# One pair's transposes on TensorE, and five weight pieces by casting DMAs, in a thresholded attention with a tanh-shrink MLP

## The chip, the cores and the metric

The kernel runs on one core of a Trainium2 chip. A core has five engines with queues of their own: TensorE (PE, with its weight loads PEld), VectorE (DVE), ScalarE (ACT), GpSimd (POOL) and SyncE (SP), which only issues DMAs here. Each engine takes its instructions in order; semaphores order the engines among each other. Sixteen DMA engines move data for all queues. The metric is the time of one execution on the device in microseconds, as a median of several runs.

## The reference, cut to what matters

```python
# q, k, v: (8, 8, 576, 64) float32; tau = 0.02
scores = (q @ k^T) / 8
thresh = max(scores, axis=-1) - tau
attn   = softmax(where(scores >= thresh, scores, -1e9))
x      = (attn @ v), heads side by side        # (4608, 512)
h      = x @ w_in                              # w_in (512, 2048)
out    = (h - tanh(h)) @ w_out                 # w_out (2048, 512)
```

## The kernel before, in words

**Attention.** The 64 (batch, head) couples are taken as 32 pairs of heads, counted from 0 in the code: the "eighth pair" is p = 7, the ninth p = 8. A pair has 2 x 576 query rows, nine tiles of 128 rows (`TPP = 9`), one of which, the shared one, holds the last 64 rows of both heads. Tiles are numbered through, i = 0 to 287; an even tile and the odd one after it make a duo. For a tile the kernel

1. computes the scores on TensorE, in PSUM (`scores`, L401 and L410). q and k are split into two float16 halves, kT holds a pair's transposed k and kS the same with the halves swapped, so that two rounds of matmuls give the float32-like product;
2. copies them to SBUF on VectorE, with the row maximum (L420), and derives the shift of a duo (`shift`, L432);
3. masks on ScalarE with a steep Prelu into z, bfloat16, the duo's two tiles side by side (`kink`, L447);
4. turns z so that keys lie on partitions. `on_pe(i)` decides: on TensorE by 128x128 transposes into PSUM (L466), four for the first tile of a duo and five for the second, each followed by an exp from PSUM (L475); or for the whole duo by one DMA transpose on SP's queue (zT, L454), followed by one exp (L483). PSUM tile psZ is double for the first four pairs and from then on shares the one buffer of psY;
5. multiplies by v on TensorE (`attend`, L506 to L524) and normalises on VectorE (`norm`). `emit_x` turns a pair's result on TensorE into xT.

**Preparation of a pair.** `load`/`load_part` bring q, k and v (up to the eighth pair on SP's queue, later on ScalarE's). `split` makes the float16 halves on GpSimd (three instructions, L228 to L232). `turn` transposes: on TensorE with a copy out of PSUM by VectorE (L284, L327), or by a DMA transpose on SP's queue (L315). `q_by_dma(p)` and `k_by_dma(p)` decide. `swap` makes kS from kT on GpSimd (two copies, L337), `split_v` casts v (L261 to L266).

**The MLP.** Per batch the hidden layer runs on TensorE in 16 steps (`hidden`, L579, psH), tanh on ScalarE (L592), the difference on VectorE (L598), and the second matrix in quarters (`project`, L605, psY). The first batch's hidden steps are mixed with the attention from step 40 on, by a written pattern.

**Weights.** w_in and w_out are loaded in eight pieces each (`w_load`): 512 KB of float32 into one of four buffers wt on SP's queue, and later a cast to bfloat16 on GpSimd (`w_cast`, L731).

**Order.** It is written out by hand: a loop over steps s = -8, -7, ... (L852) emits for each step its scores (tile s + 8), masks, turns and exps, MLP steps, attends, and then what `plan` lists for that step (loads, splits, turns, by leads before the pair's first tile: `LEADS`, `LATER`, `FIRST_LATER`), casts and weight loads. The lists `load_when` and `cast_when` hold steps counted from -8:

```python
    load_when = [3, 8, 13, 18, 21, 25, 29, 34, 38, 42, 46, 49, 52, 55, 58, 61]
    cast_when = [11, 19, 27, 32, 36, 40, 44, 47, 50, 53, 56, 59, 62, 65, 68, 71]
```

For the ninth pair `FIRST_LATER[8]` sets q's split ten, q's turn five, k's split eight and k's turn seven steps ahead.

Of the kernel before, what the change touches and what calls it, by code (L numbers as in the profile page):

```python
# [18 lines left out]
def kernel(  # L19
# [11 lines left out]
    nc = tc.nc  # L31
# [20 lines left out]
    TPP = 9  # L52
# [2 lines left out]


    def on_pe(i):
        p, j = divmod(i, TPP)
        return p < 6

    W = 2 * S

# [72 lines left out]
    DUAL = 8  # L135
# [167 lines left out]

    def q_by_dma(p):

        return p >= DUAL

    def k_by_dma(p):
        return p > DUAL
# [77 lines left out]
    def scores(i):  # L387
# [6 lines left out]
        if hh is None:  # L394
            qrem = REM
            if q_by_dma(p):
                qrem = (slice(512, 640, 2), slice(513, 640, 2))
            for n, kk in enumerate((kT, kS)):
                for dst, cols in ((main, main_keys), (rem, rem_keys)):
                    for hh in range(2):  # L400
                        nc.tensor.matmul(  # L401
                            out=ps[64 * hh : 64 * hh + 64, dst],
                            lhsT=qT[:, qrem[hh]], rhs=cols(p, kk, hh),
                            start=(n == 0), stop=(n == 1),
                        )
        else:
            lhs = qT[:, (5 * hh + t) * P : (5 * hh + t + 1) * P]
            for n, kk in enumerate((kT, kS)):
                for dst, cols in ((main, main_keys), (rem, rem_keys)):
                    nc.tensor.matmul(  # L410
                        out=ps[:, dst], lhsT=lhs, rhs=cols(p, kk, hh),
                        start=(n == 0), stop=(n == 1),
                    )
# [25 lines left out]
    def kink(i):  # L439
        sc, nb = scs.pop(i), nbs.pop(i)  # L440
        if kind(i) == "B":
            zt = zs.pop(i - 1)
            z = zt[:, S:W]
        else:
            zt = zs[i] = z_pool.tile([P, W], BF16, name="z")
            z = zt[:, 0:S]
        nc.scalar.activation(  # L447
            out=z, in_=sc, func=ACT.Prelu, bias=nb, scale=1.0, alpha=STEEP
        )
        if on_pe(i):  # L450
            zts[i] = zt
        elif kind(i) == "B":
            zts[i] = zt_pool.tile([P, TPP, P], BF16, name="zT")
            nc.sync.dma_start_transpose(out=zts[i], in_=zt)  # L454

    def weights(i):
# [4 lines left out]
        if on_pe(i):  # L461
            z = zts.pop(i)
            pl, tag = (ps_h, "h") if i % 2 and i < HPAIR * TPP else (ps_y, "y")
            ps = pl.tile([P, 5 * P], BF16, name="psZ", tag=tag)
            for c in range(n):
                nc.tensor.matmul(  # L466
                    out=ps[:, c * P : (c + 1) * P],
                    lhsT=z[:, (off + c) * P : (off + c + 1) * P],
                    rhs=ident_bf, is_transpose=True, start=True, stop=True,
                )  # L470
            if kd == "B":
                pt = pts.pop(i - 1)
            else:
                pt = p_pool.tile([P, TPP * P], FP16, name="pT")
            nc.scalar.activation(  # L475
                out=pt[:, off * P : (off + n) * P], in_=ps[:, 0 : n * P], func=ACT.Exp
            )
        elif kd == "A":
            return
        else:  # L480
            n += off
            pt = p_pool.tile([P, TPP * P], FP16, name="pT")
            nc.scalar.activation(  # L483
                out=pt[:, 0 : n * P], in_=zts.pop(i)[:, 0:n, :], func=ACT.Exp
            )
# [232 lines left out]
    def w_pieces():  # L718
        for w, sb, n in ((moe_w_in, w_in_sb, DM_C), (moe_w_out, w_out_sb, DF_C)):
            flat = sb.rearrange("p c n -> p (c n)")  # L720
            cols = n * w.shape[1] // 8
            src = w.rearrange("(c p) n -> p c n", p=P)

            for i in (0, 2, 4, 6, 1, 3, 5, 7) if w is moe_w_in else range(8):
                yield flat, src, i, cols, w.shape[1]
# [3 lines left out]
    def w_cast():  # L729
        flat, wt, i, cols = loaded.pop(0)  # L730
        nc.gpsimd.tensor_copy(out=flat[:, i * cols : (i + 1) * cols], in_=wt)  # L731

    def w_load(piece):
        flat, src, i, cols, width = piece
        wt = wt_pool.tile([P, cols], F32, name="wt", tag="wt")
        if cols >= width:
            r = cols // width
            s = src[:, i * r : (i + 1) * r, :]
            nc.sync.dma_start(out=wt.rearrange("p (c n) -> p c n", n=width), in_=s)
        else:  # L740
            r = width // cols
            s = src[:, i // r, (i % r) * cols : (i % r + 1) * cols]
            nc.sync.dma_start(out=wt, in_=s)
        loaded.append((flat, wt, i, cols))
# [53 lines left out]
    for p in range(1, DUAL):  # L798
        first = TPP * p - AHEAD
        for d, f in PREP[3 if p == 1 else 0 :]:  # L800
            d -= p == 1 and d == 3
            if p > HPAIR and d >= LDK - 2:
                d = ((16, 14, 12), (17, 15, 13))[1 - p % 2][LDK - d]
            elif d in (7, 8) and q_by_dma(p):
                d = ((9, 9) if d == 7 else (10, 10))[1 - p % 2]
            elif p in LEADS and d in (8, 7, 5, 4):
                d = LEADS[p][(8, 7, 5, 4).index(d)]
            elif d == 4:
                d = 4
            elif d == 5:  # L810
                d = k_lead(p)
            elif p in (2, 4):
                d = {8: 9, 7: 8}.get(d, d)
            plan.setdefault(first - d, []).append(lambda p=p, f=f: f(p))
        d = (6, 7)[1 - p % 2] if q_by_dma(p) else 3 - (p == 1 or p >= 5)
        d = LEADS[p][4] if p in LEADS else d
        plan.setdefault(first - d, []).append(lambda p=p: turn(p, "q"))
# [9 lines left out]
    for t in ("k", "q", "v"):  # L827
        load(1, t)
    pieces = w_pieces()
    load_when = [3, 8, 13, 18, 21, 25, 29, 34, 38, 42, 46, 49, 52, 55, 58, 61]  # L830
    cast_when = [11, 19, 27, 32, 36, 40, 44, 47, 50, 53, 56, 59, 62, 65, 68, 71]

    todo, stage = [], 0

# [17 lines left out]
    for s in range(-AHEAD, NTILE + LAG + 3):  # L852
        p, j = divmod(max(s, 0), TPP)
# [10 lines left out]
        n = s + AHEAD  # L864
# [14 lines left out]
        if s == 0:  # L879
            nc.vector.tensor_tensor(  # L880
                out=fold, in0=ident_bf[:, 0:64], in1=ident_bf[:, 64:P], op=ALU.add
# [21 lines left out]
        for _ in range(load_when.count(s + AHEAD)):  # L903
            w_load(next(pieces))
# [56 lines left out]
```

## Time and profile before

| | |
|---|---|
| median of 3 runs | 505.8 us (504.12 to 509.31) |
| span of the profiled execution | 509.7 us; no time of its own beside the span is on record |
| TensorE busy, granted clock over the span | 484.8 us (95%), 0.997 |
| VectorE, ScalarE, GpSimd busy | 400.2, 431.7, 291.4 us |
| DMA transposes on SP's queue | 117 of zT, 24 of qT, 23 of kT |
| DMA transfers | 95.32 MB, mean 187 GB/s |

Busy time is counted from an instruction's start to its end, and neighbours overlap: a matmul's time holds its passage through the array. So the mean duration of a short TensorE instruction is not what it costs in a row of its kind; the distance from start to start is. Instructions that issue DMAs are not counted as busy. In a row of a group stand the busy time, the mean duration in ns, and after the bar the idle time before these instructions with what ended it. A wait for several semaphores is put down to the one that came last.

### The profile page before, as it was taken

To read this page: it belongs to the slowest core of one execution; us is meant where nothing else is said; L and a number is where in the kernel's file an instruction comes from. 1 tells how busy PE (TensorE), PEld (TensorE's weight loads), DVE (VectorE), ACT (ScalarE), POOL (GpSimd) and SP (SyncE) were. 2 spreads that over 40 slices of the span, in tenths; PEclk is the share of its full clock that TensorE was granted. 3 is DMA by queue.
4 is the path that set the end of the run, shared out by engine and by line. 5 is a ranking of instruction groups with operands and counts; after the bars stand their busy time and mean duration, and the time that the engine had idled before them with its cause. 6 is when DMAs were issued, how large, how long until landed. Compare 5 with 4: busy or idle time off the path is not lost.

```text
span 509.7 us, 12184 instructions
## 1 busy us (share of the span) xinstructions
PE 484.8 (95%) x4283; PEld 270.9 (53%) x4345; DVE 400.2 (79%) x1150; ACT 431.7 (85%) x617; POOL 291.4 (57%) x390
## 2 busy tenths in 40 slices
PE   8999899889999989999999999999998999999997
PEld 4666566445555545555555555555554555544444
DVE  5899978878889879988898789889886887544440
ACT  5999998889999889999999999899979999533430
POOL 8999999886765375757675666569456700000000
PEclk9999999989999999999999999999999999999999
DMA  7852658999999999999999999999999986311013
GB/s 206 262 155 89 195 190 220 159 225 214 231 217 245 192 254 209 238 241 242 242 195 221 261 238 225 207 242 240 213 191 258 187 144 115 87 41 42 23 41 82
DMA packets 233341, 95.32 MB, mean 187 GB/s; under 512 B 203968, under 2 KB 222656, under 8 KB 233280
## 3 DMA queue, kind: packets, MB, share of 16 engines
q1 hardware_dynamic: 212336, 72.87, 75.1%
q10 hardware_dynamic: 20944, 21.67, 16.1%
q8 instruction: 34, 0.56, 0.5%
q14 instruction: 27, 0.22, 0.2%
HBM read 36.70 MB, written 9.44 MB: 91 GB/s over the span
## 4 chain that ended last, share of the span: by engine, by line
PE 57%; POOL 12%; DMA 9%; issue 7%; ACT 7%; DVE 5%; ACTq 1%; SPq 0%; POOLq 0%; DVEq 0%
PE psY L605 18%; PE psH L579 14%; PE psS L410 13%; DMA zT<-z 6%; PE psO L513 3%; POOL kS L337 3%; PE psHt L579 3%; ACT pT L483 3%; DMA vraw<-in_v_dram 3%; ACT z L447 2%; DVE g L598 2%; POOL qhl L232 2%; DVE sc L420 2%; PE psS L401 2%; ACTq L175 1%
## 5 line engine op out<-in xcount | busy, mean ns | idle before, releaser
L420 DVE TENSOR_SCALAR_CACHE_REDUCE sc<-psS 128x576 f32<-128x576 f32 x288 | 213.5, 752 | 27.1 <-PE psS L410 12.9
L447 ACT ACTIVATE z<-sc,nb 128x576 bf16<-128x576 f32 x288 | 216.1, 770 | 8.0 <-DVE nb L432 5.7
L483 ACT ACTIVATE pT<-zT 128x1152 f16<-128x1152 bf16 x117 | 135.2, 1155 | 12.3 <-DMA zT<-z 10.6
L605 PE MATMUL psY<-w_out_sb,g 128*128 128x512 bf16 (+1 forms) x564 | 140.8, 373 | 1.6 <-issue 0.2
L579 PE MATMUL psH<-xT,w_in_sb 128*128 128x512 bf16 x448 | 119.4, 381 | 5.1 <-issue 2.0
L337 POOL COPY kS<-kT 64x1152 f16<-64x1152 f16 x62 | 70.8, 1142 | 86.3 <-DMA kT<-khl 72.7
L598 DVE SCALAR_TENSOR_TENSOR g<-th,psH 128x512 bf16<-128x512 f32 x128 | 87.6, 685 | 33.6 <-ACT th L592 32.9
L410 PE MATMUL psS<-kT,qT 128*128 128x512 f16 (+1 forms) x512 | 104.7, 286 | 4.1 <-DVE sc L420 1.9
L410 PE MATMUL psS<-kS,qT 128*128 128x512 f16 (+1 forms) x512 | 105.1, 287 | 0.0
L410 PEld LDWEIGHTS <-qT 128*128 128x128 f16 x1024 | 72.5, 98 | 59.0 <-issue 3.8
L592 ACT ACTIVATE th<-psH 128x512 f32<-128x512 f32 x128 | 74.6, 583 | 21.4 <-PE psH L579 21.4
L605 PEld LDWEIGHTS <-g 128*128 128x128 bf16 x592 | 51.1, 98 | 54.6 <-DVE g L598 0.4
L579 PEld LDWEIGHTS <-w_in_sb 128*128 128x128 bf16 x576 | 49.4, 98 | 57.4 <-issue 6.3
L513 PE MATMUL psO<-vb,pT 128*128 128x65 bf16 x1024 | 53.3, 194 | 0.0
L513 PEld LDWEIGHTS <-pT 128*128 128x128 f16 x1024 | 44.2, 98 | 9.6
L232 POOL TENSOR_TENSOR qhl<-qraw,qhl 128x576 f16<-128x576 f32 x31 | 39.7, 1281 | 2.6
L232 POOL TENSOR_TENSOR khl<-kraw,khl 128x576 f16<-128x576 f32 x31 | 39.7, 1280 | 2.7
L475 ACT ACTIVATE pT<-psZ 128x512 f16<-128x512 bf16 (+1 forms) x54 | 35.1, 654 | 2.4 <-PE psZ L466 2.1
L506 PE MATMUL psO<-vb,pT 128*128 128x130 bf16 x128 | 28.2, 220 | 3.7 <-ACT pT L483 3.6
L617 DVE COPY yo<-psY 128x512 f32<-128x512 f32 (+1 forms) x31 | 21.1, 680 | 13.1 <-PE psY L605 12.4
L539 DVE TENSOR_TENSOR osb<-psO,rc 128x256 bf16<-128x256 f32 x64 | 27.2, 424 | 2.2
L228 POOL TENSOR_SCALAR qraw<-qraw 128x576 f32<-128x576 f32 x31 | 20.8, 671 | 11.1 <-DMA qraw<-in_q_dram 10.8
(77 smaller groups left out, 452.1 us busy)
## 6 DMA issues: line engine op xcount, KB each, us to landing
out_dram<-yo SPq DMA_DIRECT2D x32, 256.0 KB, 3.8
kraw<-in_k_dram ACTq DMA_DIRECT2D x24, 288.0 KB, 4.2
qraw<-in_q_dram ACTq DMA_DIRECT2D x24, 256.0 KB, 4.3
wt<-in_moe_w_in_dram SPq DMA_DIRECT2D x8, 512.0 KB, 4.6
wt<-in_moe_w_out_dram SPq DMA_DIRECT2D x8, 512.0 KB, 3.9
vraw<-in_v_dram ACTq DMA_DIRECT2D x24, 160.0 KB, 4.3
vraw<-in_v_dram ACTq DMA_DIRECT2D x24, 128.0 KB, 3.8
vraw<-in_v_dram SPq DMA_DIRECT2D x8, 256.0 KB, 3.6
```

The costliest lines, as they stand in the source:

```text
L232: nc.gpsimd.tensor_tensor(out=hl[:, :, 1, :], in0=x, in1=hl[:, :, 0, :], op=ALU.subtract)
L337: nc.gpsimd.tensor_copy(out=o, in_=i)
L410: nc.tensor.matmul(out=ps[:, dst], lhsT=lhs, rhs=cols(p, kk, hh), start=(n == 0), stop=(n == 1),)
L420: nc.vector.tensor_scalar(out=sc, in0=ps[:, lo : lo + S], scalar1=SC, scalar2=None, op0=ALU.mult, op1=ALU.max, accum_out=mx[:, c : c + 1],)
L447: nc.scalar.activation(out=z, in_=sc, func=ACT.Prelu, bias=nb, scale=1.0, alpha=STEEP)
L475: nc.scalar.activation(out=pt[:, off * P : (off + n) * P], in_=ps[:, 0 : n * P], func=ACT.Exp)
L483: nc.scalar.activation(out=pt[:, 0 : n * P], in_=zts.pop(i)[:, 0:n, :], func=ACT.Exp)
L513: nc.tensor.matmul(out=po[:, t - 1 + ab, :], lhsT=pt[:, blk * P : (blk + 1) * P], rhs=vb[:, hh, c, :], start=False, stop=(n == 7), skip_gr ...
L579: nc.tensor.matmul(out=ps, lhsT=w_in_sb[:, c, n * P : (n + 1) * P], rhs=xs[m][:, c, :] if m < B else xR[:, c, :, :], start=(c == 0), stop= ...
L592: nc.scalar.activation(out=th, in_=ps, func=ACT.Tanh)
L598: nc.vector.scalar_tensor_tensor(out=gs[m][:, n, :], in0=th, scalar=-1.0, in1=ps, op0=ALU.mult, op1=ALU.add,)
L605: nc.tensor.matmul(out=ps, lhsT=gs[m][:, n, ms * P : (ms + 1) * P], rhs=w_out_sb[:, n, cols], start=(n == 0), stop=(n == DF_C - 1),)
```

## The change

The tiles 62 to 71 are turned on TensorE instead of by DMA: the seventh pair's last tile, which is its shared one, and the eighth pair's nine, five duos. The seventh pair's first four duos (tiles 54 to 61) are still turned by DMA, as are all from the ninth pair on. The ninth pair's q is transposed on TensorE, with a copy by VectorE. The last five of w_out's eight pieces go by a DMA on GpSimd's queue that reads float32 and writes bfloat16 straight into w_out_sb, so they need no wt buffer and no cast; the load times of the last pieces move earlier, and `cast_when` loses its last five entries.

```diff
     def on_pe(i):
-        p, j = divmod(i, TPP)
-        return p < 6
+        return i < 6 * TPP or 62 <= i < 8 * TPP
...
     def q_by_dma(p):
 
-        return p >= DUAL
+        return p > DUAL
...
+    CASTING = 3
+
     def w_load(piece):
         flat, src, i, cols, width = piece
+        if cols >= width and i >= CASTING:
+            r = cols // width
+            nc.gpsimd.dma_start(
+                out=flat[:, i * cols : (i + 1) * cols].rearrange("p (c n) -> p c n", n=width),
+                in_=src[:, i * r : (i + 1) * r, :],
+            )
+            return
         wt = wt_pool.tile([P, cols], F32, name="wt", tag="wt")
...
-    load_when = [3, 8, 13, 18, 21, 25, 29, 34, 38, 42, 46, 49, 52, 55, 58, 61]
-    cast_when = [11, 19, 27, 32, 36, 40, 44, 47, 50, 53, 56, 59, 62, 65, 68, 71]
+    load_when = [3, 8, 13, 18, 21, 25, 29, 34, 38, 42, 45, 47, 50, 52, 54, 56]
+    cast_when = [11, 19, 27, 32, 36, 40, 44, 47, 50, 53, 56]
```

`DUAL` is 8. Because a piece of w_in is half a row of the matrix wide (`cols < width`), only w_out's pieces meet the condition. In the built program the GpSimd queue has one casting DMA ahead of the seventh pair's swap, two after the first cast of w_out, one after the second, and one after the third; all five stand before the splits of the ninth pair.

## The prediction

> **What bounds the kernel now.** I read the page first (engine shares, slices), then the table of busy time by stretch around the change, then the waits and the timelines of the engines in that stretch. The page, parts 1 and 2:
>
> ```profile
> PE 484.8 (95%) x4283; PEld 270.9 (53%) x4345; DVE 400.2 (79%) x1150; ACT 431.7 (85%) x617; POOL 291.4 (57%) x390
> ...
> PE   8999899889999989999999999999998999999997
> ...
> POOL 8999999886765375757675666569456700000000
> PEclk9999999989999999999999999999999999999999
> ```
>
> TensorE is busy 95% of the span, so what it loses early comes back at the end only if nothing later waits anyway. A slice is 12.7 us. GpSimd is full in slices 2 to 7, up to about 90 us, and TensorE has its one dip of clock in the ninth slice. The table by stretch shows the place (length, busy time of each engine, clock, DMA share, GB/s):
>
> ```profile
> 85.00:90.00 5.00, 4.60 (x52) 2.75 (x52) 4.32 (x13) 4.47 (x8) 4.79 (x7) 1.00 1.03 274
> 90.00:95.00 5.00, 4.95 (x54) 3.12 (x54) 4.92 (x15) 5.00 (x8) 2.98 (x4) 1.00 1.29 105
> 95.00:100.00 5.00, 3.73 (x41) 2.10 (x40) 4.02 (x13) 3.17 (x5) 4.72 (x7) 1.00 1.36 161
> 100.00:105.00 5.00, 2.58 (x21) 1.17 (x21) 2.27 (x7) 4.88 (x8) 4.79 (x7) 0.93 1.09 242
> 105.00:110.00 5.00, 4.86 (x27) 2.35 (x27) 3.73 (x11) 3.48 (x6) 3.17 (x6) 0.73 1.25 218
> ```
>
> From 95 to 105 us TensorE works 6.3 of 10 us, and then its granted clock falls. Who was late, in the waits of TensorE from 90 to 115 us, and in ScalarE's timeline:
>
> ```profile
> PE psO L506 <- ACT pT L483: 2.0, 2, 1.3
> PE psS L410 <- DMA qT<-qhl: 1.6, 1, 1.6
> ```
> ```profile
> 97.67 1.16 ACT L483 ACTIVATE pT<-zT 128x1152 f16<-128x1152 bf16 x1 [1.83 <-DMA zT<-z]
> ```
>
> The exp of a duo waits for its transposed tile, TensorE waits for the exp (2.0 us in two places, duos three and four of the seventh pair), and the first scores of the ninth pair wait 1.6 us for q, whose transposition SP issued at 97.63 us behind five of zT. The timeline of GpSimd shows the other end of the stretch:
>
> ```profile
> 76.22 1.28 POOL L232 TENSOR_TENSOR khl<-kraw,khl 128x576 f16<-128x576 f32 x1
> ...
> 85.24 1.04 POOL L731 CAST w_out_sb<-wt 128x1024 bf16<-128x1024 f32 x1
> ...
> 88.96 1.04 POOL L731 CAST w_out_sb<-wt 128x1024 bf16<-128x1024 f32 x1
> ...
> 91.45 1.29 POOL L232 TENSOR_TENSOR khl<-kraw,khl 128x576 f16<-128x576 f32 x1
> ```
> ```profile
> 92.95 0.67 PE L284 MATMUL ps_k<-ident_f,khl 128*128 128x128 f16 x9
> ```
>
> GpSimd ends the split of the ninth pair's k at 92.74 us and TensorE turns it at 92.95: 0.2 us of slack. The eighth pair's k is ready at 77.50 and turned at 79.92: 2.4 us.
>
> **What is removed, on the path.** Six DMA transposes: five zT from the seventh pair's last, shared tile on, and the ninth pair's q; and from the same queue the five w_out loads, two of which (issued at 82.78 and 86.31 us, 512 KB each) stand between the zT that came late. I take the wait for q (1.6) as gone for certain, the 2.0 for the exps as gone because those two duos, still turned by DMA, lose the w_out loads beside them. The clock: 0.93 and 0.73 in two stretches of 5 us is at most 0.35 + 1.35 = 1.7 us lost, gone with the gaps. Together -5.3 us. Three of the five casts (97.00, 99.35, 103.06 us) are worth nothing: GpSimd waits in that stretch anyway.
>
> **What TensorE gains in work.** Rows by shape:
>
> ```profile
> L466 PE MATMUL psZ<-ident_bf,z 128*128 128x128 bf16 x243 | 22.5, 220 | 2.3 <-ACT pT L475 1.4 <-ACT z L447 0.7
> L475 ACT ACTIVATE pT<-psZ 128x640 f16<-128x640 bf16 x27 | 19.1, 707 | 2.1 <-PE psZ L466 1.9
> L475 ACT ACTIVATE pT<-psZ 128x512 f16<-128x512 bf16 x27 | 16.2, 601 | 0.4 <-PE psZ L466 0.2
> L483 ACT ACTIVATE pT<-zT 128x1152 f16<-128x1152 bf16 x117 | 135.2, 1155 | 12.3 <-DMA zT<-z 10.6
> ```
>
> The 220 ns are one transpose's whole passage; in the timeline four psZ take 0.22 us from start to start of what follows and five 0.28, so one costs 55 ns. Five duos are 45, or 2.5 us; the nine of q, 0.50 us as ps_k takes from 92.95 to 93.45. I put all 3.0 us on the path, as TensorE is full after 105 us. The psZ share one PSUM buffer, so each turn also waits for the exp before it; from 55 to 90 us that took 1.4 us in five waits, about 0.9 us for ten tiles, which I leave to the range. ScalarE: 601 + 707 - 1155 = 153 ns a duo, 0.8 us; start to start (0.49 + 0.59 against 1.05) only 0.15. VectorE: one copy of q, 757 ns (row of L327). Both engines have gaps between 95 and 110 us, so they cost nothing there; without that cover they are at most 1.6 us, which goes into the range.
>
> The Trainium skill speaks against the transposes: "TensorE: Matmul & The Clock Gate", section "Part 4: PE-mode transpose", gives some 275 ns for one inside a kernel and says that such work does not hold the clock up as matmuls do. By that the 54 would cost 14.9 us and the total would be about 12 us slower. The trace disagrees: 55 ns from start to start, and a clock of 1.00 from 60 to 90 us, where every tile is turned so.
>
> **What GpSimd gains and loses.** It issues five DMAs, and no row shows such an issue on GpSimd. The order of the built program has them early: one ahead of the swap of the seventh pair's k (69.09 us), three among the w_out casts at 72.75, before the split of the eighth pair's k, and one after the cast at 80.18. Their data is first read by TensorE's psY steps, at 115.34 us before, some 30 us later, while SP's w_out loads landed in 3.7 us. GpSimd itself waits for none of them, but all behind them is late by their price x. Bounds: SP issues the same transfer in 0.34 us; the longest thing that GpSimd does in one helper, the swap's two copies, takes 2.33. I take 1.04, the cast of the same tile on the same engine. The five are then 5.2 us. Given back before 92.74 us: the casts at 85.24 and 88.96, 1.0 each from start to start, and the 0.36 us that GpSimd waited for kT at 81.58. So the ninth pair's k is 5.2 - 2.0 - 0.36 - 0.2 = 2.6 us late for TensorE. (4.2 - 2.4 = 1.8 of that shows already at the eighth pair's k, at 79.9 us.) TensorE takes its queue in order, so scores, attend and hidden steps behind that turn wait too.
>
> "DMA: Bandwidth & Descriptors", section "Latency and other measured facts", puts the emission of such a DMA at about 1 us. By it the lateness would be 2.4 us instead of 2.6. No run here shows it yet.
>
> **Sum.** -5.3 + 3.0 + 2.6 = +0.3 us. The durations are those of one execution with a span of 509.7 us (no other time of it is on record), above all three timed runs (504.12 to 509.31); I carry the difference over to the median: 505.8 + 0.3 = 506.1 us. A difference of 1%, 5.1 us, is about what a measurement of this kernel can tell from none.
>
> **Rivals.**
> - *GpSimd's issue is cheap* (0.34 us, as on SP). 1.7 us are less than the 2.6 given back, so nothing is late: -5.3 + 3.0 = -2.3, 503.5 us. For it: nothing is computed. Against it: none of GpSimd's copies of 128 partitions by 500 elements or more takes under 0.6 us.
> - *The stall was that execution's own.* The profiled span lies 3.9 us above the median, and from 90 to 95 us the DMA engines moved 105 GB/s at a share of 1.29, unlike any stretch near. Then the median never had the 2.0 and 1.7 us to lose: -1.6 + 3.0 + 2.6 = +4.0, 509.8 us.
> - *The pair's DMAs stay late.* The two duos whose exps waited are still turned by DMA. If the queue and not the w_out loads held them, 2.0 and perhaps the clock stay: +0.3 + 2.0 = +2.3 to +4.0, 508 to 510.
> - *Slower: GpSimd holds TensorE back.* Place: the turns of k at 79.9 and 92.95 us. The lateness is 5x - 2.6; it eats the net gain of 2.3 from x = 0.98 on, and reaches 1% from 5x - 4.9 = 5.1, x = 2.0. At the 2.33 of the swap it is 9.1 - 2.3 = +6.8, 512.6 us. For it: GpSimd is full from 62.5 to 92.7 us (28.4 of 30.2 us). Against it: part of a wait on TensorE can be covered by scores that were made ahead.
>
> **How the numbers follow.** The sum, 0.42; cheap issue, 0.16; stall not typical, 0.15; duos still late, 0.12; issue at 2 us or more, 0.15. That is 0.06 for faster by over 1% (the cheap issue, with shorter waits later on besides), 0.78 within 1%, 0.16 slower. The range reaches from 502.5 (cheap issue, less 1 us of runs' scatter) to 511.5 (short of the dearest issue).
>
> **What would show it.** Right: no wait of TensorE for qT by DMA near 104 us, clock 1.00 from 95 to 110, zT first again for the ninth pair; 54 more TensorE transposes; waits for khl at the turns of the eighth and ninth pairs' k. The time between GpSimd's instructions around the five issues gives x. Wrong: x far from 1 us, a clock that drops elsewhere, exps at about 97 us that still wait for zT, or ten tiles of the eighth pair that take more than 16 us (tiles 44 to 62, turned on TensorE, took 28.5 us between their reads of the scores, 1.58 each).

## The result, and the profile after

The changed kernel took 511.29 us (median of 17 runs, 509.03 to 515.37), the kernel before 507.23 us (17 runs, 504.12 to 515.06). The ratio is 1.008, with a 95% interval of 1.0053 to 1.0106: slower by about 4 us, clear of no change; the ratio is within 1%, the interval ends just above. Ratios here and below leave out runs that took over 1.5% longer than the fastest of the same kernel. The time lies in the stated range, 0.2 us below its upper end, and not at the 506.1 us of the likeliest case. Of these 5.2 us, 1.4 are the base: the kernel before has a median of 505.8 us in the three runs that the forecast stood on, and of 507.2 in 17.

The page of the changed kernel, engine shares and three rows of the slices (lines after 57 have a number lower by one than before; the casting DMA is L738):

```profile
PE 488.9 (95%) x4336; PEld 274.5 (53%) x4399; DVE 401.1 (78%) x1151; ACT 432.8 (84%) x622; POOL 289.8 (56%) x390
...
PE   8999898899999999999999999998999999999996
...
POOL 7999999866755684657576767466546710000000
PEclk9999999999999999999999999998999999999999
```

TensorE is as full as before. The 4.1 us that its busy time has grown by are not a measure of the added work: pages of the kernel before alone, taken later, show 484.2 to 489.6 us, with 4283 to 4345 recorded matmuls, so some records are missing. The dip of clock near 105 us is gone, but there is another one further on, where the two programs are alike. The table by stretch for the place of the change:

```profile
85.00:90.00 5.00, 4.76 (x55) 2.75 (x53) 4.28 (x13) 4.46 (x8) 4.65 (x7) 1.00 0.96 131
90.00:95.00 5.00, 4.41 (x53) 2.88 (x51) 4.42 (x14) 4.26 (x7) 3.96 (x5) 1.00 1.24 143
95.00:100.00 5.00, 4.38 (x40) 2.48 (x40) 4.94 (x13) 4.31 (x8) 3.78 (x6) 1.00 0.55 140
100.00:105.00 5.00, 3.56 (x45) 2.33 (x44) 3.29 (x11) 5.00 (x9) 4.70 (x6) 1.00 0.40 88
105.00:110.00 5.00, 4.86 (x48) 3.04 (x47) 4.39 (x13) 4.85 (x10) 3.86 (x7) 1.00 0.74 179
```

From 95 to 105 us TensorE works 7.9 us instead of 6.3, the clock stays at 1.00, and the DMA share falls to less than half. So this execution lacks the stall; whether that is the change's doing is asked in the next section. Time is lost elsewhere. GpSimd's timeline, with the five issues:

```profile
68.97 0.94 POOL L738 DMA_DIRECT2D w_out_sb<-in_moe_w_out_dram  x1
...
74.59 1.44 POOL L738 DMA_DIRECT2D w_out_sb<-in_moe_w_out_dram  x2
...
77.00 0.72 POOL L738 DMA_DIRECT2D w_out_sb<-in_moe_w_out_dram  x1
...
79.25 1.28 POOL L231 TENSOR_TENSOR khl<-kraw,khl 128x576 f16<-128x576 f32 x1
...
84.18 0.79 POOL L738 DMA_DIRECT2D w_out_sb<-in_moe_w_out_dram  x1
...
92.91 1.28 POOL L231 TENSOR_TENSOR khl<-kraw,khl 128x576 f16<-128x576 f32 x1
```

An issue takes 0.72 to 0.94 us, 3.9 us in all. The eighth pair's k is ready at 80.5 us instead of 77.5, the ninth's at 94.2 instead of 92.7. TensorE's timeline shows both turns waiting:

```profile
80.59 0.68 PE L283 MATMUL ps_k<-ident_f,khl 128*128 128x128 f16 x9 [0.50 <-POOL khl L231]
...
94.25 0.68 PE L283 MATMUL ps_k<-ident_f,khl 128*128 128x128 f16 x9 [0.43 <-POOL khl L231]
...
103.22 0.44 PE L465 MATMUL psZ<-ident_bf,z 128*128 128x128 bf16 x5 [1.39 <-ACT pT L474]
```

The third line is a wait that I had priced at some 0.9 us in total and left to the range: the transposes of a tile wait for the exp of the one before, since psZ has one buffer. In the ten tiles it comes to 1.6 us, in two waits. The longer one stands where ScalarE, which I had credited with gaps, is full (5.00 of 5 us from 100 to 105): the transposes of tile 62 are through at 101.34 us, and their exp starts at 102.59, behind an exp and a mask:

```profile
100.87 1.15 ACT L482 ACTIVATE pT<-zT 128x1152 f16<-128x1152 bf16 x1
101.92 0.76 ACT L446 ACTIVATE z<-sc,nb 128x576 bf16<-128x576 f32 x1
102.59 0.58 ACT L474 ACTIVATE pT<-psZ 128x512 f16<-128x512 bf16 x1
```

### The profile page after: what moved, and what is told of

Its sections match the earlier page's. It is cut to its first block, busy times and chain, and to the rows that moved or that the text cites. A ratio compares the mean times of both kernels' runs of the same rounds, so it can differ in the third digit from the quotient of the medians.

```text
span 513.5 us, 12270 instructions
## 1 busy us (share of the span) xinstructions
PE 488.9 (95%) x4336; PEld 274.5 (53%) x4399; DVE 401.1 (78%) x1151; ACT 432.8 (84%) x622; POOL 289.8 (56%) x390
## 4 chain that ended last, share of the span: by engine, by line
PE 59%; POOL 10%; ACT 10%; DMA 8%; issue 5%; DVE 5%; ACTq 2%; SPq 0%; POOLq 0%; DVEq 0%
PE psY L604 19%; PE psH L578 15%; PE psS L409 13%; DMA zT<-z 6%; ACT z L446 4%; PE psO L512 4%; PE psHt L578 3%; ACT pT L482 2%; PE psS L400 2%; ACT th L591 2%; DVE g L597 2%; POOL kS L336 2%; DVE sc L419 2%; ACTq L174 2%; ACT pT L474 2%
## 5 line engine op out<-in xcount | busy, mean ns | idle before, releaser
L482 ACT ACTIVATE pT<-zT 128x1152 f16<-128x1152 bf16 x112 | 129.4, 1155 | 12.4 <-DMA zT<-z 9.9
L474 ACT ACTIVATE pT<-psZ 128x512 f16<-128x512 bf16 x64 | 41.5, 651 | 2.4 <-PE psZ L465 2.0
L465 PE MATMUL psZ<-ident_bf,z 128*128 128x128 bf16 x288 | 26.7, 219 | 4.0 <-ACT pT L474 3.1
```

The costliest lines, as they stand in the source:

```text
L474: nc.scalar.activation(out=pt[:, off * P : (off + n) * P], in_=ps[:, 0 : n * P], func=ACT.Exp)
L482: nc.scalar.activation(out=pt[:, 0 : n * P], in_=zts.pop(i)[:, 0:n, :], func=ACT.Exp)
```

## What one profile can't tell: the kernel before, four times

Before the parts are taken one by one, the kernel before was run again, unchanged.

> The kernel before, unchanged, for a second profile of it. Theory A (the waits of 2.0 us for exps near 97 us and the halved clock behind them belonged to the one profiled execution): no drop of the granted clock between 95 and 110 us, TensorE busy at least 4.4 of 5 us in each stretch from 90 to 110, and the first tile of the ninth pair read before 103 us instead of at 105.0. Theory B (the stall is the kernel's own): the same waits within 1 us and tile 72 at 105 us. Time: ratio 1.000 under both, and the interval shows what this comparison can tell.

> The kernel before, unchanged, a third profile: how often the wait for zT near 97 us and the wait for q near 104 us occur. If the stall is an exception, tile 72's scores are read within 1 us of 101.8 us and the clock stays at 1.00; if it is the rule, near 105 us.

> The kernel before, unchanged, a fourth profile, for the same question as the third.

The first gave a ratio of 1.0018 (0.9982 to 1.0054) against itself: what differs by less than some 0.4% in such a comparison is not told apart. The other two were single runs (510.05 and 507.59 us). The stretches of the second profile:

```profile
95.00:100.00 5.00, 4.62 (x45) 2.50 (x43) 4.96 (x16) 4.81 (x8) 4.72 (x7) 1.00 1.12 183
100.00:105.00 5.00, 4.37 (x37) 2.35 (x35) 3.44 (x11) 5.00 (x9) 4.79 (x7) 1.00 1.01 189
105.00:110.00 5.00, 4.34 (x47) 2.65 (x46) 4.93 (x18) 4.89 (x7) 4.71 (x7) 1.00 1.24 288
```

There is no gap and no drop of the clock, and neither is there one in the third and fourth profile. To compare profiles I take the time from VectorE's read of the scores of tile 48 to that of tile 84, which spans the change (65 to about 120 us), from VectorE's timelines. The two reads in the second profile of the kernel before, and in that of the change:

```profile
65.25 0.76 DVE L420 TENSOR_SCALAR_CACHE_REDUCE sc<-psS 128x576 f32<-128x576 f32 x1
...
119.28 0.76 DVE L420 TENSOR_SCALAR_CACHE_REDUCE sc<-psS 128x576 f32<-128x576 f32 x1
```
```profile
65.21 0.76 DVE L419 TENSOR_SCALAR_CACHE_REDUCE sc<-psS 128x576 f32<-128x576 f32 x1
...
123.74 0.76 DVE L419 TENSOR_SCALAR_CACHE_REDUCE sc<-psS 128x576 f32<-128x576 f32 x1
```

| kernel | tile 48 to 84, us | against the mean of the three undisturbed | ratio of the runs (95%) |
|---|---|---|---|
| before, the profile of the prediction | 57.43 | +3.0 | |
| before, second to fourth profile | 54.03, 54.55, 54.70 | 0 (mean 54.43) | 1.0018 (0.9982 to 1.0054) for the second |
| the change | 58.53 | +4.1 | 1.008 (1.0053 to 1.0106) |
| five duos on TensorE alone | 56.54 | +2.1 | 1.0054 (1.0017 to 1.0092) |
| q on TensorE alone | 55.73 | +1.3 | 0.9985 (0.9938 to 1.0033) |
| casting DMAs alone | 55.48 | +1.1 | 1.0065 (1.0026 to 1.0103) |
| the change, casting DMAs late | 57.27 | +2.8 | 1.0061 (1.0028 to 1.0094) |
| late casting DMAs alone | 62.06 | +7.6 | 1.0172 (1.0117 to 1.0226) |
| late casting DMAs and q | 63.27 | +8.8 | 1.0152 (1.0110 to 1.0194) |
| GpSimd fills instead of DMAs | 58.51 | +4.1 | 1.0057 (1.0022 to 1.0092) |
| all pieces by casting DMAs | 54.28 | -0.2 | 1.0087 (1.0041 to 1.0132) |
| all pieces, and q | 54.96 | +0.5 | 1.0048 (1.0003 to 1.0092) |

Up to tile 56 the four profiles of the kernel before agree within 0.1 us; then DMA transposes begin, and with them the scatter. The stall that the prediction set out to remove was in one profile of four. The three others have tile 72 at 101.8 to 102.2 us instead of 105.0, as the theory of an exception had it. The late zT that began the stall is no exception of one execution, though: it comes again with q on TensorE alone, below. Behind tile 84 all kernels run the same program, and the four profiles of the kernel before alone wander apart by up to 5.6 us, more than the stall is long: the profile with the stall spans 509.7 us, the three without it 510.7, 508.2 and 505.7. So the spans of single profiles say nothing on the change, and its own in that last part (242.4 us from tile 128 to the last, against 237.3 to 240.6) no more. In the table, differences of a few tenths in the stretch say nothing either, since the undisturbed three lie 0.7 us apart.

## The parts alone

**Five duos on TensorE.**

```diff
     def on_pe(i):
-        p, j = divmod(i, TPP)
-        return p < 6
+        return i < 6 * TPP or 62 <= i < 8 * TPP
```

> Only the five duos go to TensorE; q of the ninth pair and the weight pieces as before. Theory A (TensorE's added work is on the path and the stall it was to remove was not there in most runs): 45 transposes at 55 ns, +2.5 us, ratio 1.005. Theory C (GpSimd's five DMA issues, 3.9 us by the profile, are the whole loss): 0 to -1 us, ratio 0.998 to 1.000.

Measured 1.0054, 2.7 us, and 2.1 us in the stretch: theory A, and not the 0 to -1 us of theory C. That the sum fits does not prove each summand, for the waits for the exp, 1.7 us in two places, are in it too. The second profile of the kernel before and this one record as many matmuls as weight loads (4345 and 4390), so none is missing, and TensorE's time in the stretch can be compared: busy 52.65 us against 50.70, idle 3.89 against 3.33. So some 2 us are added busy time (2.5 were forecast), and two thirds of the new waits replace other idle time.

**q of the ninth pair on TensorE.**

```diff
     def q_by_dma(p):
-        return p >= DUAL
+        return p > DUAL
```

> Only the ninth pair's q is turned on TensorE. Theory A: the wait of 1.6 us for q by DMA near 104 us goes, 0.5 us of TensorE comes: -1.1 us, ratio 0.998. Theory C: the same, the two don't differ here. If the wait was the one execution's own too: +0.5 us, ratio 1.001.

Measured 0.9985 (0.9938 to 1.0033). This can't tell -1.1 us from +0.5. Its profile had the late zT again (ScalarE waited 3.1 us for it in two places), and at the place where the prediction's profile has it (1.83 us at 97.67):

```profile
97.77 1.16 ACT L483 ACTIVATE pT<-zT 128x1152 f16<-128x1152 bf16 x1 [1.87 <-DMA zT<-z]
```

From 90 to 95 us the DMA engines moved 97 GB/s at a share of 1.16, as they moved 105 at 1.29 in the first profile, and 225 to 242 in the three undisturbed; why, is not shown. Its +1.3 us in the stretch may come from there. Tiles 62 to 72 take 13.8 us here, 15.8 in the first profile, 12.6 to 13.0 in the undisturbed: a weaker stall, without the drop of the clock. The effect of this part stays open; in the three undisturbed profiles of the kernel before, TensorE's weight loads wait 0.2, 0.3 and 0.6 us for a q by DMA between 85 and 125 us, not 1.6.

**Casting DMAs alone.** `w_load`, `load_when` and `cast_when` as in the change, `on_pe` and `q_by_dma` as before.

> Only the five weight pieces go by casting DMAs on GpSimd, at the change's load steps; z and q as before. Theory A: the eighth pair's k is ready 0.5 us and the ninth's 0.4 us late for TensorE, +1 us, ratio 1.002. Theory C: the whole loss, +4 us, ratio 1.008. If the two w_out loads beside zT were what made zT late: below 0, ratio 0.996.

Measured 1.0065 (1.0026 to 1.0103), 3.3 us, with 1.1 us in the stretch. The interval takes in neither +1 us (1.002) nor what the loads beside zT would have given (0.996), but its lower end is near the former and the stretch is at it. TensorE waited 1.2 us in three places for khl. The profile shows no further cost that would make up the rest. It may be no cost at all: by the medians of all runs this kernel has 1.0044, and the unchanged kernel run beside it 1.0040 against itself.

## Is it GpSimd's lateness, or the DMAs?

**GpSimd busy, no DMA.** Five fills of an unused tile in the places of the five issues; everything else as before.

```diff
+    extra_when = [47, 50, 52, 54, 56]
+    extra = const.tile([P, 768], BF16, name="extra")
...
+        for _ in range(extra_when.count(s + AHEAD)):
+            nc.gpsimd.memset(extra, 0.0)
         for _ in range(load_when.count(s + AHEAD)):
```

> The kernel before plus five fills of an unused tile by GpSimd (128x768, about 0.77 us each) at the places of the five casting DMAs; no casting DMA, no cast left out. Theory A (lateness of GpSimd by itself): 3.85 us of work, none given back, 0.36 us absorbed by a wait and 0.2 by slack: +3.3 us, ratio 1.0065, and TensorE waits for khl at the turns of the eighth and ninth pairs' k. Theory D: ratio 1.000 to 1.002.

Measured 1.0057, 2.9 us; 4.1 us in the stretch, a granted clock of 0.66 from 95 to 100 us, behind the wait, included. The ninth pair's k is ready at 96.00 us instead of 92.74, and TensorE's waits from 75 to 130 us name it:

```profile
94.73 1.27 POOL L232 TENSOR_TENSOR khl<-kraw,khl 128x576 f16<-128x576 f32 x1
```
```profile
PE ps_k L284 <- POOL khl L232: 2.7, 2, 2.4
```

So most of GpSimd's lateness in this stretch reaches TensorE: 3.75 us of fills, k 3.3 us late, 2.7 us of waiting for it. And the ratio, with twelve runs, shows that it reaches the end.

**The change, with the five issues late.**

```diff
-    load_when = [3, 8, 13, 18, 21, 25, 29, 34, 38, 42, 45, 47, 50, 52, 54, 56]
+    load_when = [3, 8, 13, 18, 21, 25, 29, 34, 38, 42, 45, 64, 66, 68, 70, 72]
```

> The changed kernel, with its five casting DMAs issued at steps 56 to 64, behind the split of the ninth pair's k, where GpSimd has gaps. Theory A (54 transposes on TensorE cost 3.0 us, the five issues make the splits of k 1.4 us late): the second part goes, +3.0 us against the kernel before, ratio 1.006, and no wait of TensorE for khl. Theory D (it is the casting DMAs themselves, whenever they run, that cost some 3 us): ratio 1.008 to 1.010, as the change.

Measured 1.0061 (1.0028 to 1.0094), and 2.8 us in the stretch against 4.1 of the change. In GpSimd's timeline the ninth pair's k is now split before the first issue, and ends at 90.95 us instead of 94.19:

```profile
89.67 1.28 POOL L231 TENSOR_TENSOR khl<-kraw,khl 128x576 f16<-128x576 f32 x1
90.90 0.94 POOL L738 DMA_DIRECT2D w_out_sb<-in_moe_w_out_dram  x1
```

No wait for khl is left. The two ratios overlap, so by the runs alone early and late are not told apart. The stretch and the waits are as theory A has them: 2.8 us remain where it had 3.0, and the 1.3 us less than in the change are near twice the 0.7 us by which undisturbed profiles of one kernel differ.

**Late casting DMAs alone, and with q.** The same list with `on_pe` as before; in the second kernel with q on TensorE too.

> Only the casting DMAs, at the late steps; z and q as before. Theory A: nothing is late on GpSimd, two casts of 1.0 us are gone from its full stretch: ratio 0.998 to 1.000. Theory D: ratio 1.006, as with the early casting DMAs alone.

> Late casting DMAs and the ninth pair's q on TensorE, z as before. Theory A: as the kernel with late casting DMAs, plus 0.5 us of TensorE and less the wait for q where there is one: ratio 0.997 to 1.001. Theory D: ratio 1.005.

Here both theories missed: 1.0172 and 1.0152, some 8 us. Without the five duos on TensorE, the late casting DMAs run beside the eighth pair's transposes by DMA. ScalarE's timeline and the stretches of the first of the two:

```profile
114.32 1.16 ACT L483 ACTIVATE pT<-zT 128x1152 f16<-128x1152 bf16 x1 [6.45 <-DMA zT<-z]
```
```profile
105.00:110.00 5.00, 3.96 (x37) 2.11 (x35) 4.93 (x18) 2.76 (x4) 2.91 (x5) 1.00 1.65 134
110.00:115.00 5.00, 0.00 (x0) 0.00 (x0) 0.48 (x2) 0.68 (x1) 0.00 (x0) 0.72 1.25 161
115.00:120.00 5.00, 4.46 (x32) 2.31 (x33) 1.71 (x6) 3.69 (x6) 3.16 (x4) 0.60 1.23 237
```

One exp waits 6.45 us for its transposed tile, TensorE does nothing for five microseconds, and the clock drops. What the DMA queues did from 109 to 112 us (packets, MB, time of the packets as a share of 16 engines):

```profile
q0 software_dynamic: 180, 0.18, 116.9%
q1 hardware_dynamic: 132, 0.03, 24.7%
```

q0 is GpSimd's queue, q1 SP's with the transposes. GpSimd's packets fill the engines and move little; the transposes' packets take a quarter of the engines' time. The second kernel waits 6.1 us in the same way. In the change with late issues, where the eighth pair's duos are turned on TensorE, no exp waits for zT from 75 to 130 us; and issued early, as above, the same five DMAs cost 1.1 us in the stretch. So in these runs casting DMAs were dear where zT was due beside them. Why these packets are slow stays open: stretches of full engines and little data occur without casting DMAs too (105 GB/s at a share of 1.29 from 90 to 95 us in the first profile of the kernel before).

## A version that beats both?

Two kernels took all sixteen pieces by casting DMAs, w_in too, with z by DMA as before, q by DMA or on TensorE.

```diff
     def w_load(piece):
         flat, src, i, cols, width = piece
+        if cols < width:
+            r = width // cols
+            nc.gpsimd.dma_start(
+                out=flat[:, i * cols : (i + 1) * cols],
+                in_=src[:, i // r, (i % r) * cols : (i % r + 1) * cols],
+            )
+            return
...
+    load_when = [3, 7, 11, 15, 19, 22, 25, 28, 31, 34, 37, 40, 43, 45, 47, 49]
+    cast_when = []
```

> A version that might beat both: z and q as in the kernel before; all sixteen weight pieces by casting DMAs, spread from step -5 to 41, before the first DMA transpose. GpSimd's full stretch loses 13 casts of 1.0 us ahead of the ninth pair's k and gets 16 issues of 0.72 to 0.94 us, so its end moves little (+0.5 us at 0.78 each, -2 us if a w_in piece, with half as many runs of memory, is issued in 0.6), and no weight load stands beside zT. If the loads beside zT cause the wait for zT near 97 us: no such wait, and ratio 0.995 to 1.000. If the lateness of GpSimd decides: ratio 1.000 to 1.003.

> The same, and the ninth pair's q on TensorE (0.5 us of TensorE, one DMA transpose less in SP's queue). Where zT is not late, 0.5 us slower than the kernel with all pieces by casting DMAs; where it is, up to 1.1 us faster. Ratio 0.994 to 1.002.

1.0087 (1.0041 to 1.0132) and 1.0048 (1.0003 to 1.0092): no gain. The first lies outside both of its expected ranges, the second's interval reaches into its own. The first loses 1.5 us before tile 16, where the first issues push GpSimd's work back (TensorE waits 1.1 us for kS and 0.8 for khl between 10 and 30 us), and wins none of it back: from tile 16 to tile 48 its reads of the scores keep the distance to those of the kernel before within 0.02 us, although a w_in issue takes 0.53 to 0.61 us where the cast took 1.04. GpSimd, now with gaps, waits itself:

```profile
83.45 2.32 POOL L337 COPY kS<-kT 64x1152 f16<-64x1152 f16 x2 [2.82 <-DVE nb L432]
```

So from tile 16 to tile 48 GpSimd was full without setting the pace. The rest of the measured loss is not explained by the profile, in which the stretch of the change is the shortest but one of all. A cost of casting DMAs that shows in no stretch, 2 to 3 us here and with the five alone, is neither shown nor excluded; the change could have it too.

## Why the prediction was right or wrong, point by point

**What bounds the kernel: half right.** TensorE's full share was the right frame: the work added to it came back at the end. The stall at 95 to 108 us was real in the profile that I read, and three of four profiles of the kernel lack it; the late zT alone, with a weaker stall, came once more, with q on TensorE.

**The saving of 5.3 us: wrong, and the step that failed.** "I take the wait for q (1.6) as gone for certain" and the 2.0 and 1.7 us beside it are not in an undisturbed execution. Of the 5.3 us some 0.2 to 0.6, of the wait for q, were there to save in three profiles of four. The rival that doubted it had the right suspicion from the wrong sign: a span is no time (in later runs of this kernel the time is 1.9 us above the span, so that execution lay some 5.8 us above the median, not 3.9), and a long span is no mark of the stall, for the second profile spans 510.7 us without one. Only more profiles tell. The saving ought to have been weighted, by a quarter as it turned out.

**TensorE's 3.0 us: right in size, not in its parts.** 2.7 us for the duos alone (0.9 to 4.7 by the interval), 2.8 us in the stretch for duos and q with the issues late. The 55 ns from start to start held (0.23 us for four of them, from 100.95 us on), but only some 2.0 of the duos' 2.5 us show as added busy time; the rest is waiting, for an exp that ScalarE had no gap for. The clock stayed at 1.00 through these transposes. The Trainium skill's 275 ns ("TensorE: Matmul & The Clock Gate", section "Part 4: PE-mode transpose") would have made it 14.9 us instead of 3.0; these runs don't agree with it as a cost in a row of transposes. What it says of the clock is not tested, for the transposes here stand among matmuls.

**The price of an issue: mis-sized, the mechanism right.** 1.04 us taken, 0.78 measured (0.72 to 0.94). With it the prediction's own 5x - 2.6 gives 1.3 us: the ninth pair's k was ready 1.45 us later (94.19 against 92.74) and turned 1.30 us later (94.25 against 92.95), instead of 2.6. Both turns of k waited for khl, as named. The fills show that such lateness goes to the end. The rival of a cheap issue fails at the same price; its 0.34 us is the shortest issue of a w_in load, while SP's w_out loads took 0.37 to 0.54.

**The rival that held** was the stall of that execution alone, +4.0 us. It had a chance of 0.15, and its number holds by luck, for two errors cancel: it kept the 1.6 us for q, most of which was not there either, and had 2.6 us of lateness for 1.3. With the measured terms the sum is 3.0 + 1.3, less 0.2 to 0.6, or 3.7 to 4.1 us; 4.1 us were measured, in the stretch and by the ratio (0.8% of 507.2 us, 2.7 to 5.4). That it fits so closely is luck too, given 0.7 us of scatter in the stretch and the open effect of q.

**The rival of duos that stay late** did not show: in the profile of the change one exp of the seventh pair waits 0.7 us for its zT, and the clock is 1.00 from 95 to 110 us. It could not be told from the first, since the wait comes and goes.

**The slower rival,** GpSimd holding TensorE back from 0.98 us an issue on, had the right place and the wrong threshold: it counted against a saving that was not there.

## What to carry to other kernels

Look at a second and a third profile of the same kernel before pricing a stall, whatever its span: a wait that hangs on DMA timing may come in one execution and not in the next, while work added to the engine that is full was paid here in every kernel that had the five duos. A transposition moved from a DMA to a full TensorE costs at least some of its start-to-start time, and waits of its own, and buys only what the DMA was really late. A DMA issued by GpSimd was here an instruction of that engine of 0.5 to 0.9 us, harmless to TensorE where the engine has gaps, and its transfer was dear where transposes of z by DMA were due.

## What the runs showed of the hardware that was not expected

- An issue of a casting DMA holds GpSimd for 0.53 to 0.61 us with 128 runs of 4 KB (one early one 0.77) and for 0.71 to 0.94 us with 256 runs of 2 KB.
- Casting DMAs landed after a median of 5.1 us in the change (SP's plain loads of w_out's pieces before, 3.9 us), and after 9.5 us for the four that ran beside transposes of z by DMA.
- The granted clock falls at other places in other executions, where the kernels run the same instructions: near 350 us in the profile of the change (0.66 from 350 to 355 us, behind a stretch with 3.8 us of work in five), and between 155 and 160 us in that of the duos alone (0.68). Both times ScalarE had just waited 3.0 us in two places for zT.
